# Linear attention and a squared-ReLU MLP on one core: MLP batches of 576 columns in fixed slots with attention pieces, instead of attention first and MLP in chunks of 512

## The chip, the cores and the metric

The kernel runs on one core of a Trainium2 chip. The metric is the device time of one execution in microseconds (us); the median of three runs of the kernel before is 393.43 us (390.52 to 395.26). The engines are TensorE (PE for its matmuls, PEld for its weight loads), VectorE (DVE), ScalarE (ACT), GpSimd (POOL) and SyncE (SP). SP and POOL issue the DMAs here; the data itself is moved by 16 DMA engines.

## The reference

Linear attention over 8 batches, 8 heads, 576 positions and head size 64, and then an MLP over the 4608 tokens with 512 model and 2048 inner columns:

```
theta = pi/2 * pos / S;  c, s = cos(theta), sin(theta)
phi(x) = concat(relu(x)*c, relu(x)*s)            # 64 -> 128 features
q_p, k_p = phi(q), phi(k)
kv  = einsum('bhsf,bhsd->bhfd', k_p, v)           # 128 x 64 per head
z   = sum(k_p, axis=2)
x   = (q_p @ kv) / (q_p @ z + 1e-6)               # heads side by side: 4608 x 512
out = relu(x @ w_in)**2 @ w_out                   # 512 -> 2048 -> 512
```

All inputs and the output are float32 in HBM; the kernel multiplies in bfloat16 and adds up in float32.

## The kernel before, in words

The program is written as two loops, one over the 8 batches of attention (`attention_batch`, L138) and one over 9 chunks of 512 tokens of the MLP (`mlp_chunk`, L277). Its framework orders the instructions by priority, so MLP chunks start as soon as their columns of `xT` are there, and both are mixed until the attention runs out.

A batch has 576 positions: four slices of 128 rows (position 4p+j is row p of slice j) and a tail slice of 64 rows. `attention_batch` loads K, V and Q by SP (L141 to L192), each a block of 1 MB and a tail of 128 KB. Per slice it makes the features of K, the cosine half on DVE (L167) and the sine half on ACT (L175), and casts V on ACT into `vext` (L181), which has a column of ones beside each head so that z comes out of the same matmul. For each head the five slices are then added up in PSUM by five matmuls in a row (kz, L203), and the sums are copied to `kvz` (L210). Per slice of Q it makes the features (L215, L223), transposes the 8 heads on TensorE against an identity (tps, L231), copies them out of PSUM (qpT, L235), multiplies by `kvz` (numh, L244, 65 columns per head, in two halves of 4 heads), divides (L252 adds epsilon, L259 inverts, L260 multiplies) and transposes the result in four blocks on TensorE again (L268) into `xT` (L273). `xT` holds all 4608 columns.

`mlp_chunk` computes 16 blocks of 128 inner columns (hps, L283, four matmuls of 512 columns each), applies relu on ACT (rt, L291) and squares on DVE (gT, L292). Then four output tiles of 128 tokens each take 16 matmuls of 512 columns (yps, L298), a copy on ACT (ysb, L306) and a store by SP (L313).

The weights are loaded and cast to bfloat16 by two DMAs of POOL at the very start (L104, L107). PSUM has two buffers for each of the four uses. SP issues its DMAs in order, so that a load which waits for its buffer holds up the ones behind it.

Of the kernel before, what the change touches and what calls it, by code (L numbers as in the profile page):

```python
# [9 lines left out]
ALU = mybir.AluOpType  # L11
ACTF = mybir.ActivationFunctionType
# [3 lines left out]
TOK_CHUNK = 512  # L16
EPS = 1e-06
PS_SMALL_BUFS = 2
PS_T_BUFS = 2
PS_H_BUFS = 2  # L20
PS_Y_BUFS = 2
ROWS_PER_PART = 4
# [3 lines left out]
def kernel(  # L26
# [12 lines left out]
    assert P == 128 and H * D == 512 and D == 64  # L39
    F = 2 * D  # L40
    DM, DFF = moe_w_in.shape
    T = B * S
    NB = DM // P
    KB = NB
    HB = DFF // P
    CH = max(c for c in range(P, TOK_CHUNK + 1, P) if T % c == 0)
    assert T % CH == 0 and CH % P == 0
    NCH = T // CH
    NTT = CH // P
    HH = H // 2  # L50

    J = min(ROWS_PER_PART, S // P)
    assert J >= 1
    MAIN = J * P
    TAIL = S - MAIN
    assert 0 <= TAIL < P
    NSL = J + (1 if TAIL > 0 else 0)
# [3 lines left out]
    xpool = ctx.enter_context(tc.tile_pool(name="xTp", bufs=1))  # L61
    inp = ctx.enter_context(tc.tile_pool(name="inp", bufs=2))
    kvb = ctx.enter_context(tc.tile_pool(name="kvb", bufs=2))
    qwork = ctx.enter_context(tc.tile_pool(name="qwork", bufs=2))
    small = ctx.enter_context(tc.tile_pool(name="small", bufs=2))
    mlp = ctx.enter_context(tc.tile_pool(name="mlp", bufs=2))
    ypool = ctx.enter_context(tc.tile_pool(name="ypool", bufs=2))
    ps_small = ctx.enter_context(
        tc.tile_pool(name="ps_small", bufs=PS_SMALL_BUFS, space=bass.MemoryType.PSUM)
    )  # L70
    ps_t = ctx.enter_context(tc.tile_pool(name="ps_t", bufs=PS_T_BUFS, space=bass.MemoryType.PSUM))
    ps_h = ctx.enter_context(tc.tile_pool(name="ps_h", bufs=PS_H_BUFS, space=bass.MemoryType.PSUM))
    ps_y = ctx.enter_context(tc.tile_pool(name="ps_y", bufs=PS_Y_BUFS, space=bass.MemoryType.PSUM))

    ident = const.tile([P, P], BF16, name="ident")
    make_identity(nc, ident)
    sidx = const.tile([P, J + 1], F32, name="sidx")
    nc.gpsimd.iota(
        sidx[:, 0:J],
        pattern=[[1, J]],  # L80
        base=0,
        channel_multiplier=J,
        allow_small_or_imprecise_dtypes=True,
    )
    nc.gpsimd.iota(
        sidx[:, J : J + 1],
        pattern=[[1, 1]],
        base=MAIN,
        channel_multiplier=1,
        allow_small_or_imprecise_dtypes=True,  # L90
    )
    cos_col = const.tile([P, J + 1], F32, name="cos_col")
    sin_col = const.tile([P, J + 1], F32, name="sin_col")
    bias_pi2 = const.tile([P, 1], F32, name="bias_pi2")
    nc.vector.memset(bias_pi2, math.pi / 2.0)
    theta_scale = (math.pi / 2.0) / S
    nc.scalar.activation(
        cos_col, sidx, ACTF.Sin, bias=bias_pi2[:], scale=-theta_scale
    )
    nc.scalar.activation(sin_col, sidx, ACTF.Sin, bias=0.0, scale=theta_scale)  # L100
# [3 lines left out]
    nc.gpsimd.dma_start(  # L104
        out=w1sb[:, :, :], in_=moe_w_in.rearrange("(kb p) f -> p kb f", p=P)
    )
    nc.gpsimd.dma_start(  # L107
        out=w2sb[:, :, :], in_=moe_w_out.rearrange("(hb p) f -> p hb f", p=P)
    )

    xT = xpool.tile([P, NB, T], BF16, name="xT")

    slices = [(j, P) for j in range(J)] + ([(J, TAIL)] if TAIL > 0 else [])

    def xT_dest(b, j, rows):
        c0 = b * S + (j * P if j < J else MAIN)
        return xT[:, :, c0 : c0 + rows]

    def col_to_token_pieces(c0: int, n: int):
        pieces = []  # L120
        col = c0
        end = c0 + n
        while col < end:
            b = col // S
            u = col - b * S
            if u >= MAIN:
                cnt = min(end - col, S - u)
                pieces.append((col - c0, b * S + u, 1, cnt))
                col += cnt
            else:  # L130
                j = u // P
                p0 = u % P
                cnt = min(end - col, P - p0)
                pieces.append((col - c0, b * S + J * p0 + j, J, cnt))
                col += cnt
        return pieces

    def attention_batch(b: int):  # L138
        Kb = inp.tile([P, H, J, D], F32, name="Kb", tag="Kb", bufs=2)
        Vb = inp.tile([P, H, J, D], F32, name="Vb", tag="Vb", bufs=2)  # L140
        nc.sync.dma_start(  # L141
            out=Kb[:, :, :, :],
            in_=k[b, :, 0:MAIN, :].rearrange("h (p j) d -> p h j d", j=J),
        )
        nc.sync.dma_start(
            out=Vb[:, :, :, :],
            in_=v[b, :, 0:MAIN, :].rearrange("h (p j) d -> p h j d", j=J),
        )
        if TAIL > 0:
            Kt = inp.tile([P, H, D], F32, name="Kt", tag="Kt", bufs=2)  # L150
            Vt = inp.tile([P, H, D], F32, name="Vt", tag="Vt", bufs=2)
            nc.sync.dma_start(
                out=Kt[:TAIL],
                in_=k[b, :, MAIN:S, :].rearrange("h p d -> p h d"),
            )
            nc.sync.dma_start(  # L156
                out=Vt[:TAIL],
                in_=v[b, :, MAIN:S, :].rearrange("h p d -> p h d"),
            )

        kp = kvb.tile([P, NSL, H, F], BF16, name="kp", tag="kp", bufs=2)
        vext = kvb.tile([P, NSL, H, D + 1], BF16, name="vext", tag="vext", bufs=2)
        nc.vector.memset(vext[:, :, :, D : D + 1], 1.0)
        for j, rows in slices:
            ksrc = Kb[:rows, :, j, :] if j < J else Kt[:rows, :, :]
            vsrc = Vb[:rows, :, j, :] if j < J else Vt[:rows, :, :]
            nc.vector.tensor_scalar(  # L167
                out=kp[:rows, j, :, 0:D],
                in0=ksrc,
                scalar1=0.0,  # L170
                scalar2=cos_col[:rows, j : j + 1],
                op0=ALU.max,
                op1=ALU.mult,
            )
            nc.scalar.activation(  # L175
                out=kp[:rows, j, :, D:F],
                in_=ksrc,
                func=ACTF.Relu,
                scale=sin_col[:rows, j : j + 1],
            )  # L180
            nc.scalar.copy(out=vext[:rows, j, :, 0:D], in_=vsrc)  # L181

        Qb = inp.tile([P, H, J, D], F32, name="Qb", tag="Qb", bufs=1)
        nc.sync.dma_start(
            out=Qb[:, :, :, :],
            in_=q[b, :, 0:MAIN, :].rearrange("h (p j) d -> p h j d", j=J),
        )
        if TAIL > 0:
            Qt = inp.tile([P, H, D], F32, name="Qt", tag="Qt", bufs=2)
            nc.sync.dma_start(  # L190
                out=Qt[:TAIL],
                in_=q[b, :, MAIN:S, :].rearrange("h p d -> p h d"),  # L192
            )

        kvz = kvb.tile([P, H, D + 1], BF16, name="kvz", tag="kvz", bufs=2)
        for half in range(2):
            kz = ps_small.tile(
                [P, HH, D + 1], F32, name="kz", tag="psm", bufs=PS_SMALL_BUFS
            )
            for hh in range(HH):  # L200
                h = half * HH + hh
                for ji, (j, rows) in enumerate(slices):
                    nc.tensor.matmul(  # L203
                        out=kz[:, hh, :],
                        lhsT=kp[:rows, j, h, :],
                        rhs=vext[:rows, j, h, :],
                        start=(ji == 0),
                        stop=(ji == len(slices) - 1),
                    )
            nc.scalar.copy(out=kvz[:, half * HH : half * HH + HH, :], in_=kz[:, :, :])  # L210

        for j, rows in slices:
            qsrc = Qb[:rows, :, j, :] if j < J else Qt[:rows, :, :]
            qp = qwork.tile([P, H, F], BF16, name="qp", tag="qp", bufs=2)
            nc.vector.tensor_scalar(  # L215
                out=qp[:rows, :, 0:D],
                in0=qsrc,
                scalar1=0.0,
                scalar2=cos_col[:rows, j : j + 1],
                op0=ALU.max,  # L220
                op1=ALU.mult,
            )
            nc.scalar.activation(  # L223
                out=qp[:rows, :, D:F],
                in_=qsrc,
                func=ACTF.Relu,
                scale=sin_col[:rows, j : j + 1],
            )
            tps = ps_t.tile([P, H, P], BF16, name="tps", tag="tps", bufs=PS_T_BUFS)
            for h in range(H):  # L230
                nc.tensor.transpose(  # L231
                    tps[:, h, :rows], qp[:rows, h, :], ident[:rows, :rows]
                )
# [81 lines left out]
    for b in range(B):  # L315
        attention_batch(b)
    for c in range(NCH):
        mlp_chunk(c)
# [30 lines left out]
```

## Time and profile before

| what | value |
|---|---|
| median of three runs | 393.43 us (390.52 to 395.26) |
| span of the profiled execution, first to last instruction | 388.8 us |
| granted TensorE clock, mean | 0.973 of full |
| TensorE, VectorE, ScalarE busy | 335.3, 173.0, 185.3 us |
| matmuls | 2272: 1152 of the MLP, 1120 of attention |
| DMA packets | 45755, 42.32 MB, mean 109 GB/s |

The profiled execution's own time is not listed apart from its span; the three runs lie 1.7 to 6.5 us above that span, the median 4.6. Busy time of TensorE is the union of its matmuls, of which each is recorded with its way through the array (about 0.2 us more than its step to the next one), so the step between starts is the better measure of cost. "Releaser" is what ended an engine's wait. A few per cent of the matmul records are missing.

### The profile page before, as it was taken

What the parts mean: (1) busy time and instruction counts of PE and PEld (TensorE: products, weight loads), DVE (VectorE), ACT (ScalarE), POOL (GpSimd) and SP (SyncE); (2) the same over time, 40 slices, a digit from 0 to 9 for tenths busy, and PEclk for the clock granted to TensorE, in tenths of its full rate; (3) what the DMA queues carried; (4) which work ended last, traced back from release to release, by engine and by line L of the source; (5) the groups of instructions that cost most, each with busy time, mean ns of one, the idle gap of its engine ahead of it and who ended that gap; (6) DMA issues with size and microseconds to landing.
All of it is one profiled execution on the core that took longest, in us unless ns stands there. A gap on an engine that the chain in (4) does not pass through costs nothing.

```text
span 388.8 us, 5849 instructions
## 1 busy us (share of the span) xinstructions
PE 335.3 (86%) x2272; PEld 173.0 (44%) x2272; DVE 173.0 (44%) x553; ACT 185.3 (48%) x319; POOL 2.9 (1%) x10
## 2 busy tenths in 40 slices
PE   0014586999999797999999999999999999999995
PEld 0013444565555454655544444444444444444442
DVE  1002757879687888584870150240330420420410
ACT  1063718689565758323642461551551642633621
POOL 3000000000000000000000000000000000000000
PEclk9999999899899698999999999999999999999999
DMA  8999861958859424242001101202102103002013
GB/s 218 225 214 304 258 200 25 362 198 253 248 166 306 131 78 139 65 127 66 1 2 52 57 0 54 56 0 64 46 0 83 27 6 77 28 27 79 4 27 83
DMA packets 45755, 42.32 MB, mean 109 GB/s; under 512 B 13984, under 2 KB 40608, under 8 KB 45728
## 3 DMA queue, kind: packets, MB, share of 16 engines
q1 hardware_dynamic: 43136, 37.76, 32.7%
q0 software_dynamic: 2592, 4.19, 5.8%
q8 instruction: 18, 0.29, 0.3%
q14 instruction: 9, 0.07, 0.1%
HBM read 36.70 MB, written 9.44 MB: 119 GB/s over the span
## 4 chain that ended last, share of the span: by engine, by line
PE 79%; DVE 8%; DMA 6%; SPq 2%; issue 2%; ACT 1%; ACTq 0%
PE yps L298 32%; PE hps L283 31%; DMA Qb<-in_q_dram 6%; PE tps L231 5%; PE kz L203 4%; PE tps L268 3%; PE numh L244 3%; DVE qpT L235 2%; SPq L156 2%; DVE attn L260 1%; DVE kp L167 1%; DVE qp L215 1%; DVE xT L273 1%; DVE den L252 1%; ACT vext L181 1%
## 5 line engine op out<-in xcount | busy, mean ns | idle before, releaser
L283 PE MATMUL hps<-xT,w1sb 128*128 128x512 bf16 x576 | 138.2, 389 | 0.5 <-DVE xT L273 0.5
L298 PE MATMUL yps<-w2sb,gT 128*128 128x512 bf16 x576 | 132.7, 382 | 1.6 <-DVE gT L292 0.8
L292 DVE TENSOR_TENSOR gT<-rt 128x512 bf16<-128x512 bf16 x144 | 60.4, 420 | 129.3 <-ACT rt L291 128.3
L291 ACT ACTIVATE rt<-hps 128x512 bf16<-128x512 f32 x144 | 85.3, 596 | 46.9 <-PE hps L283 45.0
L298 PEld LDWEIGHTS <-gT 128*128 128x128 bf16 x576 | 55.2, 98 | 63.8 <-issue 1.8
L283 PEld LDWEIGHTS <-w1sb 128*128 128x128 bf16 x576 | 55.3, 100 | 61.9 <-issue 4.6
L306 ACT COPY ysb<-yps 128x512 f32<-128x512 f32 x36 | 21.0, 585 | 84.0 <-PE yps L298 83.8
L203 PE MATMUL kz<-vext,kp 128*128 128x65 bf16 (+1 forms) x320 | 26.4, 204 | 27.7 <-ACT kp L175 22.5
L223 ACT ACTIVATE qp<-Qb,sin_col 128x512 bf16<-128x512 f32 x32 | 22.9, 719 | 27.8 <-PE tps L231 13.3
L203 PEld LDWEIGHTS <-kp 128*128 128x128 bf16 (+1 forms) x320 | 18.5, 100 | 34.6 <-ACT kp L175 24.6
L231 PE MATMUL tps<-ident,qp 128*128 128x128 bf16 (+1 forms) x320 | 29.3, 236 | 4.1 <-ACT qp L223 4.1
L260 DVE TENSOR_TENSOR attn<-numh,rden 128x256 bf16<-128x256 f32 (+1 forms) x80 | 32.1, 414 | 0.2
L268 PE MATMUL tps<-ident,attn 128*128 128x128 bf16 (+1 forms) x160 | 23.2, 232 | 9.6 <-DVE attn L260 9.4
L235 DVE COPY qpT<-tps 128x1024 bf16<-128x1024 bf16 (+1 forms) x40 | 25.3, 634 | 11.8 <-PE tps L231 11.3
L181 ACT CAST vext<-Vb 128x512 bf16<-128x512 f32 x32 | 18.4, 611 | 18.6 <-DMA Vb<-in_v_dram 18.6
L231 PEld LDWEIGHTS <-qp 128*128 128x128 bf16 (+1 forms) x320 | 21.9, 109 | 5.8 <-ACT qp L223 4.2
L268 PEld LDWEIGHTS <-attn 128*128 128x128 bf16 (+1 forms) x160 | 12.5, 103 | 25.8 <-DVE attn L260 17.6
L244 PE MATMUL numh<-kvz,qpT 128*128 128x65 bf16 (+1 forms) x320 | 18.7, 204 | 5.7 <-DVE qpT L235 5.7
L244 PEld LDWEIGHTS <-qpT 128*128 128x128 bf16 (+1 forms) x320 | 14.8, 107 | 19.0 <-DVE qpT L235 15.3
L175 ACT ACTIVATE kp<-Kb,sin_col 128x512 bf16<-128x512 f32 x32 | 21.7, 713 | 0.5 <-DMA Kb<-in_k_dram 0.5
L273 DVE COPY xT<-tps 128x512 bf16<-128x512 bf16 (+1 forms) x40 | 15.8, 394 | 11.5 <-PE tps L268 11.3
L215 DVE TENSOR_SCALAR qp<-Qb,cos_col 128x512 bf16<-128x512 f32 x32 | 15.1, 476 | 10.4 <-DMA Qb<-in_q_dram 10.4
(24 smaller groups left out, 74.0 us busy)
## 6 DMA issues: line engine op xcount, KB each, us to landing
Kb<-in_k_dram SPq DMA_DIRECT2D x8, 1024.0 KB, 7.8
Vb<-in_v_dram SPq DMA_DIRECT2D x8, 1024.0 KB, 10.8
Qb<-in_q_dram SPq DMA_DIRECT2D x8, 1024.0 KB, 5.5
out_dram<-ysb SPq DMA_DIRECT2D x40, 128.0 KB, 2.3
out_dram<-ysb SPq DMA_DIRECT2D x16, 256.0 KB, 2.4
w1sb<-in_moe_w_in_dram POOLq DMA_DIRECT2D x1, 2048.0 KB, 17.9
w2sb<-in_moe_w_out_dram POOLq DMA_DIRECT2D x1, 2048.0 KB, 32.2
Kt<-in_k_dram SPq DMA_DIRECT2D x8, 128.0 KB, 8.9
```

The lines of the kernel that those rows point to most:

```text
L181: nc.scalar.copy(out=vext[:rows, j, :, 0:D], in_=vsrc)
L203: nc.tensor.matmul(out=kz[:, hh, :], lhsT=kp[:rows, j, h, :], rhs=vext[:rows, j, h, :], start=(ji == 0), stop=(ji == len(slices) - 1),)
L223: nc.scalar.activation(out=qp[:rows, :, D:F], in_=qsrc, func=ACTF.Relu, scale=sin_col[:rows, j : j + 1],)
L231: nc.tensor.transpose(tps[:, h, :rows], qp[:rows, h, :], ident[:rows, :rows])
L235: nc.vector.tensor_copy(out=qpT[:, :, :rows], in_=tps[:, :, :rows])
L244: nc.tensor.matmul(out=numh[:rows, hh, :], lhsT=qpT[:, h, :rows], rhs=kvz[:, h, :], start=True, stop=True,)
L260: nc.vector.tensor_tensor(out=attn[:rows, half * HH : half * HH + HH, :], in0=numh[:rows, :, 0:D], in1=rden[:rows].unsqueeze(2).to_broadca ...
L268: nc.tensor.transpose(tps2[:, blk, :rows], attn[:rows, 2 * blk : 2 * blk + 2, :], ident[:rows, :rows],)
L283: nc.tensor.matmul(out=hps[:, :], lhsT=w1sb[:, kb, hb * P : (hb + 1) * P], rhs=xT[:, kb, t0 : t0 + CH], start=(kb == 0), stop=(kb == KB - 1),)
L291: nc.scalar.activation(out=rt[:, :], in_=hps[:, :], func=ACTF.Relu)
L292: nc.vector.tensor_tensor(out=gT[:, hb, :], in0=rt[:, :], in1=rt[:, :], op=ALU.mult)
L298: nc.tensor.matmul(out=yps[:, :], lhsT=gT[:, hb, tt * P : (tt + 1) * P], rhs=w2sb[:, hb, :], start=(hb == 0), stop=(hb == HB - 1),)
```

## The change

The whole of it is written out in one fixed order per engine (`manual_schedule`), which is the program's own.

The MLP goes by batches of 576 columns. A *slot* is a piece of MLP on TensorE. Batch b has nine slots of gemm1: four for columns 0 to 255 (four inner blocks each, matmuls of 256 columns), four for columns 256 to 511, one for the tail (16 inner blocks, matmuls of 64 columns). Each has one relu and one square over 1024 columns. Then come eight slots of gemm2 (8 matmuls of 512 columns, half an output tile each); the tails of batches 2i and 2i+1 share one output tile, in two further slots after the odd one. Batch 0 adds up four output tiles at once, so that it can use the second weight piece by piece. After each slot stand the attention pieces that a plan puts there: features of K and V casts, kz in two parts, features of Q, num with its division, all for the batch one or two ahead. For batch b from 4 on, with o and p the first slots of batches b-2 and b-1: K and V features at slots o+9 to o+11, kz at o+12 and o+13, Q features at o+13 to o+15, num and division at p+4 to p+8.

Further edits:

- kz runs slice by slice over all heads, in one PSUM buffer of two banks that num and the transposes of x share.
- num and division are done for all 8 heads at once (one of each DVE instruction instead of two).
- The transposes of Q's features and of x stay on TensorE for batches 0 and 1. For batches 2 to 7 they are DMAs issued by SP, one for a pair of slices and one for the tail: six a batch.
- V's cast moves from ACT to DVE; the copy out of the x transposes that stay on TensorE moves from DVE to ACT.
- K, V and Q of batch 0 come first, on SP. A copy of one head of V on POOL stands ahead of the weights, which come in four pieces each: the first weight, batch 1 (q, k, v), the second weight, batch 2, all on POOL. Batch 3 follows on POOL at slot 15. From batch 4 on, SP loads K and V at slot 35 or at slot 15 of batch b-3, and Q at o+9.
- Output stores go by POOL, those of the last batch by SP.
- Matmuls without a use (`warm`, `fill`) run on TensorE while it waits at the start.

The diff, cut to its core:

```diff
-    nc.gpsimd.dma_start(
-        out=w1sb[:, :, :], in_=moe_w_in.rearrange("(kb p) f -> p kb f", p=P)
-    )
...
+    def att_kv(b, part):
...
+        for j, rows in slices[:2] if part == 0 else slices[2:]:
             for hh in range(HH):
...
+                for half in range(2):
                     h = half * HH + hh
                     nc.tensor.matmul(
+                        out=kz[:, half, hh * E1 : (hh + 1) * E1],
+                        lhsT=kp[:rows, j, h, :],
+                        rhs=vx[:rows, j, h, :],
+                        start=(j == 0 and hh == 0),
+                        stop=(j == J and hh == HH - 1),
                     )
...
+    def att_qT(b, i):
...
+        nc.sync.dma_start_transpose(
+            out=t[:, :, :], in_=qps[b, i][:rows].rearrange("p r h f -> p (r h f)")
+        )
...
+    def att_num(b, j, early=False):
...
+            num = ps_a.tile([P, 2, FP], F32, name="num", tag="pa", bufs=1)
...
+    def att_x(b, i):
...
+        nc.sync.dma_start_transpose(
+            out=xT.rearrange("p k (r c) -> p (k r) c", r=n),
+            in_=xs[b, i][:rows].rearrange("p k r c -> p (k r c)"),
+        )
...
+    def gemm1(b, s):
...
+        half = s // 4
+        w, nh = (2 * P, 4) if half < 2 else (TAIL, HB)
+        h0 = s % 4 * nh
+        hps = ps_h.tile([P, nh, w], F32, name="hps", tag="hps", bufs=2)
+        xT = xT_of(b, half)
...
+        step = P if (b, s) == (0, 0) else w
+        for c in range(0, w, step):
+            for i in range(nh):
+                hb = h0 + i
+                for kb in range(KB):
+                    nc.tensor.matmul(
+                        out=hps[:, i, c : c + step],
+                        lhsT=w1sb[:, kb, hb * P : (hb + 1) * P],
+                        rhs=xT[:, kb, c : c + step],
+                        start=(kb == 0),
+                        stop=(kb == KB - 1),
+                    )
+        rt = mlp.tile([P, nh, w], BF16, name="rt", tag="rt", bufs=2)
+        nc.scalar.activation(out=rt[:, :, :], in_=hps[:, :, :], func=ACTF.Relu)
...
+    def gemm2(b, s):
...
+        tt, part = divmod(s, 2)
+        if part == 0:
+            yps = ps_y.tile([P, DM], F32, name="yps", tag="yps", bufs=2)
+            ypss[b] = yps[:, :]
+        for hb in range(part * HB // 2, (part + 1) * HB // 2):
+            gemm2_mm(b, tt, hb, ypss[b])
+        if part == 1:
+            store(b, tt, ypss[b])
...
+    at(15, load_batch, 3, nc.gpsimd, "qkv")
+    plan(
+        2,
+        k=(26, 26, 27, 27, 28),
+        f=(18, 20, 22, 26, 26),
+        kv=(29, 29),
+        d=(30, 31, 32, 33, 34),
+    )
...
+    for b in range(4, B):
+        o, p = first[b - 2], first[b - 1]
+        at(35 if b == 4 else first[b - 3] + 15, load_batch, b, nc.sync, "kv")
+        at(o + 9, load_batch, b, nc.sync, "q")
+        plan(
+            b,
+            k=(o + 9, o + 9, o + 10, o + 10, o + 11),
+            f=(o + 13, o + 13, o + 14, o + 14, o + 15),
+            kv=(o + 12, o + 13),
+            d=[p + 4 + j for j in range(NS)],
+        )
+
+    def run(s):
+        fn, b, i = slots[s]
+        rest = fn(b, i)
+        for fn2, args in after.get(s, []):
+            fn2(*args)
+        if rest:
+            rest()
...
+    with tc.manual_schedule():
+        load_batch(0, nc.sync, "kvq")
+        constants()
...
+        att_v(0, J - 1, nc.gpsimd, H - 1, H)
...
+        for i in range(4):
+            load_w1(i, 4)
+        load_batch(1, nc.gpsimd, "qkv")
+        for i in range(4):
+            load_w2(i, 4)
+        load_batch(2, nc.gpsimd, "qkv")
+        att_kv(0, 0)
+        att_kv(0, 1)
...
+        for s in range(len(slots)):
+            run(s)
```

`run` issues a slot's matmuls and relu, then its attention pieces, then its square.

More of the change, by code (lines that the diff above doesn't have):

```diff
@@ L6 @@
 import concourse.tile as tile
-from concourse import bass_utils, mybir
+from concourse import mybir
 from concourse._compat import with_exitstack
@@ L138, in attention_batch @@
[L138 to L143, printed above, removed]
-        )
-        nc.sync.dma_start(
-            out=Vb[:, :, :, :],
-            in_=v[b, :, 0:MAIN, :].rearrange("h (p j) d -> p h j d", j=J),
-        )
[L149 to L154, printed above, removed]
-            )
-            nc.sync.dma_start(
-                out=Vt[:TAIL],
-                in_=v[b, :, MAIN:S, :].rearrange("h p d -> p h d"),
-            )
[L161 to L199, printed above, removed]
-            for hh in range(HH):
[L201 to L233, printed above, removed]
-            qpT = qwork.tile([P, H, P], BF16, name="qpT", tag="qpT", bufs=2)
-            nc.vector.tensor_copy(out=qpT[:, :, :rows], in_=tps[:, :, :rows])
-            attn = qwork.tile([P, H, D], BF16, name="attn", tag="attn", bufs=2)
-            for half in range(2):
-                numh = ps_small.tile(
-                    [P, HH, D + 1], F32, name="numh", tag="psm", bufs=PS_SMALL_BUFS
-                )
-                for hh in range(HH):
@@ new lines, in att_qT_pe @@
+    def att_qT_pe(b, j, apart=False):
+        rows = slices[j][1]
+        tq = ps_y.tile([P, H, P], BF16, name="tq", tag="yps", bufs=2)
+        if apart:
+            hi = ps_h.tile([P, HH, P], BF16, name="tqh", tag="hps", bufs=2)
+        else:
+            hi = tq[:, HH:H, :]
+        tqs[b, j] = [tq[:, 0:HH, :], hi]
+        for h in range(H):
+            nc.tensor.transpose(
+                tqs[b, j][h // HH][:, h % HH, :rows], qp_of(b, j)[:rows, h, :], ident[:rows, :rows]
+            )
@@ new lines, in att_qT_copy @@
+    def att_qT_copy(b, j, both=False):
+        rows = slices[j][1]
+        qpTs[b, j] = [
+            att.tile([P, HH, P], BF16, name=f"qpTp{i}", tag=f"qpTp{i}", bufs=5) for i in range(2)
+        ]
+        for i, t in enumerate(qpTs[b, j]):
+            copy = nc.scalar.copy if both and i else nc.vector.tensor_copy
+            copy(out=t[:, :, :rows], in_=tqs[b, j][i][:, :, :rows])
+    def att_num(b, j, early=False):
+        rows = slices[j][1]
+        qpT, kvz = qpTs[b, j], kvzs[b]
+        if early:
+            num = ps_h.tile([P, 2, FP], F32, name="num", tag="hps", bufs=2)
+        else:
+            num = ps_a.tile([P, 2, FP], F32, name="num", tag="pa", bufs=1)
+        for h in range(H):
+            e0 = (h % HH) * E1
+            nc.tensor.matmul(
+                out=num[:rows, h // HH, e0 : e0 + E1],
+                lhsT=qpT[h // HH][:, h % HH, :rows],
+                rhs=kvz[:, h, :],
+                start=True,
+                stop=True,
+            )
+        nums[b, j] = num
@@ new lines, in store @@
+    def store(b, tt, acc):
+        ysb = mlp.tile([P, DM], F32, name="ysb", tag="ysb", bufs=4)
+        nc.scalar.copy(out=ysb[:, :], in_=acc)
+        eng = nc.sync if b == B - 1 else nc.gpsimd
+        if tt < J:
+            rows = [(0, P, b * S + tt, J)]
+        else:
+            rows = [(k * TAIL, TAIL, (b - 1 + k) * S + MAIN, 1) for k in range(2)]
+        for p0, n, row0, step in rows:
+            dst = bass.AP(tensor=out.tensor, offset=row0 * DM, ap=[[step * DM, n], [1, DM]])
+            eng.dma_start(out=dst, in_=ysb[p0 : p0 + n, :])
@@ new lines, with at, att_d, att_t @@
+    NS = J + 1
+    slots, first = [], {}
+    for b in range(B):
+        first[b] = len(slots)
+        slots += [(gemm1, b, i) for i in range(9)]
+        slots += [(gemm2, b, i) for i in range(2 * J + (2 if b % 2 else 0))]
+    after = {}
+    def at(s, fn, *args):
+        after.setdefault(s, []).append((fn, args))
+    def att_d(b, j):
+        att_num(b, j)
+        att_div(b, j)
+    def att_t(b, j):
+        att_qT_pe(b, j)
+        att_qT_copy(b, j)
+    def att_v_dve(b, j):
+        att_v(b, j, nc.vector)
```

423 lines of the change are left out of this document (279 added, 144 removed).

## Prediction

> **What bounds the kernel now.** I read the page first, then busy time by stretches, the waits of TensorE, the chain of waits, and last a few places of the timeline for the price of each kind of matmul.
>
> ```profile
> span 388.8 us, 5849 instructions
> PE 335.3 (86%) x2272; PEld 173.0 (44%) x2272; DVE 173.0 (44%) x553; ACT 185.3 (48%) x319; POOL 2.9 (1%) x10
> ```
>
> ```profile
> 0.00:22.54 22.54, 0.00 (x1) 0.01 (x1) 1.92 (x7) 2.98 (x6) 2.95 (x10) 1.00 0.97 219
> 22.54:52.40 29.86, 13.52 (x128) 9.95 (x129) 13.86 (x46) 15.80 (x27) 0.00 (x0) 1.00 1.04 280
> 52.40:162.00 109.60, 99.41 (x927) 57.93 (x926) 86.07 (x300) 74.44 (x132) 0.00 (x0) 0.92 0.58 177
> 162.00:204.80 42.80, 42.74 (x388) 23.87 (x388) 29.69 (x104) 17.77 (x30) 0.00 (x0) 0.96 0.18 51
> 204.80:384.40 179.60, 179.58 (x833) 81.22 (x830) 41.45 (x98) 73.75 (x124) 0.00 (x0) 1.00 0.15 40
> ```
>
> Columns of the second fence: stretch and its length, then busy time of PE, PEld, DVE, ACT and POOL, granted TensorE clock, DMA share, GB/s. Four stages are to be seen: 22.5 us in which TensorE has nothing, 30 us in which it is busy for less than half, 152 us in which attention and MLP are mixed, and 180 us of pure MLP without a gap at clock 1.00.
>
> A busy TensorE isn't one at its peak, so I price each kind of matmul by the step from one start to the next. A group of n that lasts L, with about 0.2 us for one of it, has the step (L - 0.2)/(n - 1).
>
> ```profile
> 204.81 13.81 PE yps L298 x64
> 370.57 13.83 PE yps L298 x64
> ...
> 162.28 0.27 PE L203 MATMUL kz<-vext,kp 128*128 128x65 bf16 x3
> ...
> 162.28 2.56 PE L203 MATMUL kz<-vext,kp 128*128 128x65 bf16 x34
> 164.78 0.62 PE L231 MATMUL tps<-ident,qp 128*128 128x128 bf16 x8
> 169.20 0.43 PE L244 MATMUL numh<-kvz,qpT 128*128 128x65 bf16 x8
> 178.47 0.44 PE L244 MATMUL numh<-kvz,qpT 128*64 128x65 bf16 x8
> ```
>
> - 512 columns: 13.81/64 = 0.2158 us, for both matrix products of the MLP.
> - 128 columns (transposes): (0.62 - 0.22)/7 = 0.057 us. A line through these two gives 0.110 for 256 columns.
> - 65 columns: kz 0.035, numh 0.033 us (with 64 columns of weights 0.034), though each loads weights of its own. kz adds into the same place up to five times in a row, and that costs nothing.
> - But 34 kz in a row take (2.56 - 0.2)/33 = 0.072 us each, not 0.035. Every fifth has 64 rows instead of 128, so one head takes 5 x 0.072 = 0.36 us instead of 0.175: going to the short tile and back costs about 0.1 us each time.
>
> By these steps the whole kernel needs 1152 x 0.2158 + 64 x 0.36 + 320 x 0.036 + 480 x 0.055 = 248.6 + 23.0 + 11.5 + 26 = 309 us on TensorE. The span holds 22.5 us ahead of the first matmul, 4.4 behind the last, and so 53 us of waits and slow clock, nearly all before 162 us. The longest of them:
>
> ```profile
> PE kz L203 <- ACT kp L175: 22.5, 1, 22.5
> PE tps L268 <- DVE attn L260: 9.4, 10, 1.1
> PE numh L244 <- DVE qpT L235: 5.7, 9, 1.1
> ```
>
> **The change, part by part.** The profiled execution stands at 388.8 us of span against a median of 393.4, so I work in span and add 4.6 us.
>
> *Start.* K, V and Q of batch 0 now go first on SP, and the weights wait on POOL behind a copy that reads V.
>
> ```profile
> 6.96 1.67 DVE L167 TENSOR_SCALAR kp<-Kb,cos_col 128x512 bf16<-128x512 f32 x4 [5.70 <-DMA Kb<-in_k_dram]
> 21.24 0.62 ACT L181 CAST vext<-Vb 128x512 bf16<-128x512 f32 x1 [18.59 <-DMA Vb<-in_v_dram]
> 35.31 0.88 DVE L215 TENSOR_SCALAR qp<-Qb,cos_col 128x512 bf16<-128x512 f32 x2 [10.20 <-DMA Qb<-in_q_dram]
> ...
> 2.00:6.00 4.00, 0.00 (x0) 0.00 (x0) 0.00 (x0) 0.63 (x3) 1.57 (x2) 1.00 0.91 279
> 36.00:40.00 4.00, 2.33 (x23) 1.92 (x24) 2.95 (x11) 2.62 (x6) 0.00 (x0) 1.00 1.09 385
> 40.00:42.00 2.00, 1.20 (x16) 0.94 (x13) 1.42 (x3) 1.13 (x2) 0.00 (x0) 1.00 0.68 165
> ```
>
> Before, K was there at 7 us, V only at 21 and Q at 35, since both shared the queues' turns with the weights. K, V and Q of a batch are 3 x 1.18 MB; at 279 to 385 GB/s from 2 us on, V lands at 8 to 10 us and Q at 11 to 15, or near 20 if the weights take turns with it again. kz then runs at 12 to 15 us. Behind Q come features, transposes, copies, num, division, x transposes and copy for two slices, 5 to 6 us by the durations below and the cold steps. The first MLP slot starts at 19 to 26 us; I take 21.
>
> *TensorE's work.* gemm1 on 256 columns: 1024 x 0.110 = 112.6. Its tails, 512 matmuls of 64 columns: nearest is the 65-column step, 0.030 to 0.036, so 15 to 18; I take 16.4 (before, these columns cost 13.8). gemm2: 576 x 0.2158 = 124.3. kz now goes slice by slice over all heads, so the short tile is met once a batch and not once a head: 40 x 0.035 + 0.2 = 1.6, times 8 = 12.8, a gain of 10. num 11.5. Transposes on TensorE are left for batches 0 and 1 alone: 120 x 0.056 = 6.7, a gain of 20. Sum 284.3, of which 3.8 lie ahead of the first slot: 280.5.
>
> *What goes beside it.* Between two slots stand attention pieces, each with a change of tile and a semaphore. Bounds: nothing, and 0.25 us for each of ten pieces a batch, 20 us; the mixed stretch at 162 to 204.8 shows PE busy throughout, so I take 6. ACT and DVE must keep up:
>
> ```profile
> L291 ACT ACTIVATE rt<-hps 128x512 bf16<-128x512 f32 x144 | 85.3, 596 | 46.9 <-PE hps L283 45.0 <-DVE gT L292 0.7 <-DVE rden L259 0.5
> L292 DVE TENSOR_TENSOR gT<-rt 128x512 bf16<-128x512 bf16 x144 | 60.4, 420 | 129.3 <-ACT rt L291 128.3 <-ACT vext L181 0.8
> L260 DVE TENSOR_TENSOR attn<-numh,rden 128x256 bf16<-128x256 f32 x64 | 25.8, 415 | 0.2
> L223 ACT ACTIVATE qp<-Qb,sin_col 128x512 bf16<-128x512 f32 x32 | 22.9, 719 | 27.8 <-PE tps L231 13.3 <-DMA Qb<-in_q_dram 11.0 <-DVE xT L273 2.3
> L259 DVE RECIPROCAL rden<-den 128x4 f32<-128x4 f32 x64 | 10.2, 169 | 0.0
> L252 DVE TENSOR_SCALAR den<-numh 128x4 f32<-128x4 f32 x64 | 9.1, 159 | 4.9 <-PE numh L244 3.9
> ```
>
> A batch takes TensorE 280.5/8 = 35 us. ACT has 9 relus of 1024 (at most 2 x 0.596), ten features of 0.72, five output copies and one of kvz: 22 us. DVE has 9 squares (0.84), ten features, five V copies and five divisions: about 21. Both fit. The tight place is the five gemm1 slots that carry a division: DVE 0.16 + 0.17 + 2 x 0.415 + 0.84 = 2.0 us against 16 x 0.110 + 8 x 0.033 = 2.02 on TensorE.
>
> *Transposes by DMA.* From batch 2 on a batch sends 1.77 MB of qp and x through SP in six DMAs, in order with its loads. The trace holds no transposing DMA. As large pieces at 385 GB/s they would take 4.6 us a batch, as small pieces at 165 GB/s (40 to 42 us, where the 128 KB tails go in rows of 256 B) 10.7; with 3.5 MB of loads (9 us) and 1.2 MB of stores (3 us) that is 17 to 23 us of the DMA engines in 35. Latency: x of a pair leaves five slots (9 us) ahead of its use in batch 2 and twelve later. So I price them at nothing; the cover is these slots, and gone it costs what the rival below says.
>
> *Weights.* First 2 MB, then batch 1, then the second 2 MB, on POOL.
>
> ```profile
> w1sb<-in_moe_w_in_dram POOLq DMA_DIRECT2D x1, 2048.0 KB, 17.9
> w2sb<-in_moe_w_out_dram POOLq DMA_DIRECT2D x1, 2048.0 KB, 32.2
> ```
>
> Both together took 32 us beside other loads, so about 13 each alone. From 11 us: w1 until 24 to 29, batch 1 until 33 to 44, w2 until 46 to 58. TensorE asks for the first piece of w2 near 43 us and for the last near 53. Late by 0 to 15 us; I take 4.
>
> *End.*
>
> ```profile
> 384.46 0.59 ACT L306 COPY ysb<-yps 128x512 f32<-128x512 f32 x1 [2.87 <-PE yps L298]
> ```
>
> The same copy and store stand last: 4.4 us. **Sum:** 21 + 280.5 + 6 + 4 + 4.4 = 316 us of span, 320 with 4.6 around it.
>
> **The rivals.**
>
> *DVE paces the division slots.* num has a single PSUM buffer, so slot s+1 can't write num before the division of s is through, and that division stands behind a square. If a slot loses 0.5 us, 5 x 8 x 0.5 = 20 us: 340. For it: 2.0 against 2.02. Against it: 30 of 35 us where DVE is slack.
>
> *Loads arrive late at the start.* w2 and batch 2 come 15 us late instead of 4, the start at 26 instead of 21: 336. For it: a DMA share near 1 up to 52 us. Against it: the order asks for less at a time.
>
> *The clock.* If unbroken work brings the 0.92 of 52 to 162 us, 280.5/0.92 adds 24: 344. Against it: 1.00 through 180 us of unbroken matmuls.
>
> *Transposing DMAs are slow; the other side.* Neighbouring elements of a row go to different partitions. If that splits the writes, the DMA engines bound six batches. Pieces of 64 B that each take as long as one of 256 B would move 165/4 = 41 GB/s: 43 us a batch, 55 with loads and stores, and 50 us ahead of them, six batches and a last MLP of 35 give 50 + 6 x 55 + 35 = 415, 420 with 4.6: slower. It decides from 39 us a batch (50 + 6 x 51 + 35 = 391) on; half as bad, 30 us, gives 50 + 6 x 42 + 35 = 337, 342 in all. For it: no row prices such a write. Against it: up to 23 us a batch it is hidden altogether, a margin of two over the row for small pieces.
>
> The Trainium skill differs from itself on this. Its page "VectorE: DVE Perf Modes", section "The three transpose paths", gives 1309 ns for a 128x128 block by DMA against 390 by TensorE; a batch's 51 blocks one behind the other would be 67 us, an estimate, and the sum 50 + 6 x 79 + 35 = 559, deep in the slower case. Its page "DMA: Bandwidth & Descriptors", section "Latency and other measured facts", gives 261 GB/s for a transposing DMA, 6.8 us a batch, an estimate, which would be hidden and leave the sum as it is. The trace shows neither; it shows TensorE's transposes at a step of 57 ns.
>
> *The change does less than it says:* TensorE is spared 25 us of work (309 to 284) and waits as long as before: 393 - 25 = 368. For it: fixed slots are still a chain of waits. Against it: the waits quoted above are on features and division of the same slice, and the slots put a whole slot of MLP between such steps.
>
> **How the numbers follow.** The forecast 0.68; DVE 0.10; loads 0.08; clock 0.03; slow transposes 0.08, of which 0.05 slower than before; less than it says 0.03. The forecast's own ends: with kz and tails at 0.030, 19 + 276 + 0 + 0 + 4.4 + 4.6 = 304, and 26 + 282 + 14 + 8 + 4.4 + 4.6 = 339. The range 304 to 346 takes in the first, the loads, the clock and most of DVE. A measurement here tells about 1% from no change; faster by that 0.93, within it 0.02, slower 0.05.
>
> **What would show it.** Right: first MLP matmul near 21 us; TensorE without gaps over 0.3 us from 60 us on; groups of 64-column matmuls at 0.03 us; kz at 1.6 us a batch; no wait of TensorE on a DMA behind 60 us. Wrong: TensorE waiting for qpT or xT from a DMA in batches 2 to 7; num waiting for the division; granted clock under 0.97 behind 60 us; gemm1 steps over 0.115.

## The result, and the profile after

The changed kernel takes 303.95 us (median of 4 runs, 303.73 to 304.23) against 391.98 us before: ratio 0.7755, interval 0.7712 to 0.7797. The forecast was 320 with a range of 304 to 346, so the direction and most of the size were right and the time lies 0.05 us under the lower end. The profiled execution took 304.11 us, with a span of 302.3.

The head of the page of the changed kernel:

```profile
span 302.3 us, 6836 instructions
PE 289.0 (96%) x2911; PEld 201.7 (67%) x2911; DVE 140.3 (46%) x330; ACT 157.8 (52%) x214; POOL 42.5 (14%) x69
PE   0899999999999999999999999999999999999993
PEclk9999999999999999999999999999999999999998
```

TensorE is busy in every slice from the second to the last but one, at a granted clock of 0.9 or more. The stretches, with the columns as in the prediction, cut at the first MLP slot, at 60 us and at the tail slots of batches 2 and 4 (two stretches between them look the same and are left out):

```profile
0.00:19.86 19.86, 11.07 (x111) 6.27 (x112) 8.69 (x24) 10.79 (x18) 8.72 (x18) 1.00 0.97 240
19.86:60.00 40.14, 40.14 (x464) 30.16 (x462) 22.79 (x56) 23.54 (x35) 14.81 (x20) 1.00 1.09 303
60.00:111.23 51.23, 51.23 (x563) 38.19 (x562) 32.23 (x78) 32.43 (x45) 3.93 (x8) 1.00 0.74 181
...
179.87:297.80 117.93, 117.90 (x1096) 78.81 (x1092) 43.06 (x95) 53.02 (x68) 8.64 (x14) 1.00 0.43 112
```

Behind 19.86 us there is no stretch in which TensorE is idle. All its waits on other engines, over the whole execution:

```profile
PE wm L185 <- ACT kp L163: 7.2, 1, 7.2
PE kz L214 <- DVE vext L177: 1.0, 1, 1.0
PE num L277 <- ACT qpTp L266: 0.2, 1, 0.2
```

All three lie ahead of the first slot. Of the 86.5 us of span that are gone (388.8 - 302.3), 53 are the waits and the slow clock of the old mixed stage, 6 the start (22.5 us; now 19.9, in which 3.8 us of work are done) and 27 work that TensorE no longer has (309 us; now 277.9 behind the start and those 3.8). How the 53 us divide among the edits is not shown: no kernel here leaves the fixed order out. The steps of its matmuls, from the chain of waits (MLP) and from the timeline (attention):

```profile
280.51 17.28 PE yps L384 x80
128.82 8.73 PE hps L351 x80
143.82 1.87 PE hps L351 x64
```

```profile
120.32 0.65 PE L214 MATMUL kz<-vext,kp 128*128 128x65 bf16 x16
120.81 1.89 PE L384 MATMUL yps<-w2sb,gT 128*128 128x512 bf16 x8
122.54 1.00 PE L214 MATMUL kz<-vext,kp 128*128 128x65 bf16 x24
123.47 0.82 PE L384 MATMUL yps<-w2sb,gT 128*128 128x512 bf16 x3
```

17.28/80 = 0.216 us for 512 columns, 8.73/80 = 0.109 for 256, 1.87/64 = 0.029 for 64. kz takes 0.49 and 0.93 us to the start of the next group, 1.42 a batch. num takes 0.26 us a slice and 0.38 for the tail. Counted out behind the first slot, 1008 matmuls of 256 columns (110.0 us), 32 of 128 (1.8), 512 of 64 (15.0), 576 of 512 (124.4), kz of seven batches (9.9), 38 num (10.8) and the 88 transposes that are left (4.6, an estimate from 0.056 for a full one) make 276.5 of the 277.9 us.

The transposing DMAs, and a stretch in which only one of them, for an x pair, moved data (last columns: DMA share, GB/s):

```profile
qpT<-qp SPq DMA_TRANSPOSE x12, 3.9
xT<-x SPq DMA_TRANSPOSE x12, 3.4
qpT<-qpt SPq DMA_TRANSPOSE x6, 3.5
xTt<-xt SPq DMA_TRANSPOSE x6, 2.3
```

```profile
246.00:249.00 3.00, 3.00 (x58) 2.81 (x56) 2.31 (x8) 1.74 (x2) 0.00 (x0) 1.00 0.48 92
```

A pair of slices lands 3.4 to 3.9 us behind its issue. 92 GB/s at a share of 0.48 is 192 GB/s of a full share: by this, an estimate, 1.77 MB would hold the DMA engines for 9.2 us a batch, between the 4.6 and 10.7 of the prediction, and with loads and stores for some 21 of 35.

### The profile page after: what moved, and what is told of

Same layout as the page of the kernel before. It is cut to its first block, busy times and chain, and to the rows that moved or that the text cites. A ratio compares the mean times of both kernels' runs of the same rounds, so it can differ in the third digit from the quotient of the medians.

```text
span 302.3 us, 6836 instructions
## 1 busy us (share of the span) xinstructions
PE 289.0 (96%) x2911; PEld 201.7 (67%) x2911; DVE 140.3 (46%) x330; ACT 157.8 (52%) x214; POOL 42.5 (14%) x69
## 4 chain that ended last, share of the span: by engine, by line
PE 93%; DMA 3%; SPq 1%; ACT 1%; DVE 0%; issue 0%; ACTq 0%
PE hps L351 42%; PE yps L384 39%; PE num L277 4%; PE kz L214 3%; DMA q<-in_q_dram 3%; PE yh L384 2%; PE tq L255 1%; SPq L69 1%; PE tx L323 1%; PE wm L197 0%; ACT qpTp L266 0%; SPq L65 0%; DVE qp L153 0%; ACT ysb L372 0%; PE tqh L255 0%
## 5 line engine op out<-in xcount | busy, mean ns | idle before, releaser
L351 PEld LDWEIGHTS <-w1sb 128*128 128x128 bf16 x1552 | 114.2, 98 | 12.4
L351 PE MATMUL hps<-xT,w1sb 128*128 128x256 bf16 (+1 forms) x1040 | 117.7, 271 | 0.0
L384 PE MATMUL yps<-w2sb,gT 128*128 128x512 bf16 x480 | 109.4, 379 | 0.0
L359 ACT ACTIVATE rt<-hps 128x1024 bf16<-128x1024 f32 x72 | 73.7, 1024 | 59.4 <-DVE gT L366 32.8
L366 DVE TENSOR_TENSOR gT<-rt 128x1024 bf16<-128x1024 bf16 x64 | 44.0, 687 | 83.8 <-ACT rt L359 83.8
L372 ACT COPY ysb<-yps 128x512 f32<-128x512 f32 x34 | 19.9, 589 | 57.2 <-PE yps L384 57.2
L380 POOL DMA_DIRECT2D out_dram<-ysb x34 | 20.6, 609 | 187.1 <-ACT ysb L372 187.1
L163 ACT ACTIVATE qp<-q,sin_col 128x512 bf16<-128x512 f32 x32 | 21.9, 717 | 4.1 <-DMA q<-in_q_dram 4.1
L163 ACT ACTIVATE kp<-k,sin_col 128x512 bf16<-128x512 f32 x32 | 21.2, 715 | 3.5 <-DMA k<-in_k_dram 3.5
L295 DVE TENSOR_TENSOR x<-num,rden 128x512 bf16<-128x512 f32 x32 | 22.1, 692 | 1.1
L351 PE MATMUL hps<-xTt,w1sb 128*128 128x64 bf16 x512 | 16.2, 193 | 0.0
```

Source lines behind the costliest of these rows:

```text
L163: nc.scalar.activation(out=dst[:rows, :, D:F], in_=src, func=ACTF.Relu, scale=sin_col[:rows, j : j + 1])
L295: nc.vector.tensor_tensor(out=x_of(b, j)[:rows].rearrange("p (b k) (l d) -> p b k l d", b=2, l=2), in0=n4[:, :, :, 0:D].rearrange("p b (k ...
L351: nc.tensor.matmul(out=hps[:, i, c : c + step], lhsT=w1sb[:, kb, hb * P : (hb + 1) * P], rhs=xT[:, kb, c : c + step], start=(kb == 0), sto ...
L359: nc.scalar.activation(out=rt[:, :, :], in_=hps[:, :, :], func=ACTF.Relu)
L366: nc.vector.tensor_tensor(out=dst, in0=rt[:, :, :], in1=rt[:, :, :], op=ALU.mult)
L372: nc.scalar.copy(out=ysb[:, :], in_=acc)
```

## The experiments

Theory: behind the start, the time is the sum of TensorE's steps, changes of tile included, and everything else is hidden. Each rival says that something else holds it up, or that some of TensorE's work is hidden. The kernels ran in three groups, each on one chip; the last group had the changed kernel with it. Times are set against 303.95 us, in the last group against 303.84.

**Transposes of batches 4 to 7 back on TensorE.**

```diff
-            d=[p + 4 + j for j in range(NS)],
+            d=(p + 2, p + 4, p + 6, p + 8, p + 10),
+            t=(p, p + 1, p + 2, p + 3, p + 5),
+            x=(p + 3, p + 5, p + 7, p + 9, p + 11),
```

> The changed kernel with the transposes of qp and x of batches 4 to 7 on TensorE again, as it does them for batch 1, in place of 24 transposing DMAs. Theory (TensorE's steps alone make the time behind 20 us): each batch gets 40 transposes of qp and 20 of x back, 32 x 0.056 + 8 x 0.042 + 16 x 0.056 + 4 x 0.055 = 3.2 us, four batches 13 us, so 317 against 303.95. Rival (transposing DMAs hold up something themselves, so that leaving them out gives time back): under 312. Rival (the copies out of PSUM load DVE and ACT so far that they pace): over 321.

317.63 us, 13.7 more; the theory said 13. (num and division also move, to every second slot.) So the DMAs take this work off TensorE at no price of their own, and the extra copies out of PSUM are hidden.

**kz head by head in its second part.**

```diff
-        for j, rows in slices[:2] if part == 0 else slices[2:]:
-            for hh in range(HH):
-                for half in range(2):
+        for hh in range(HH):
+            for half in range(2):
+                for j, rows in part_slices:
```

> The changed kernel, but in the second part of kz each head adds up its three slices before the next head begins, so that the 64-row tile is met 8 times a batch and not once. Same 320 matmuls, same sums. Theory (every TensorE step is on the path, and a change between 128 and 64 rows costs 0.095 to 0.1 us): 7 more pairs of changes a batch, 7 x 2 x 0.097 = 1.36 us, for seven batches 9.5 and up to 1.4 more at the start: 314. Rival (the slots have room beside TensorE's work, kz is hidden): 304.

317.18 us (315.64 to 318.53), 13.2 more where 10 were expected. The timeline of one batch:

```profile
126.00 0.65 PE L215 MATMUL kz<-vext,kp 128*128 128x65 bf16 x16
...
128.22 2.46 PE L215 MATMUL kz<-vext,kp 128*128 128x65 bf16 x24
130.61 4.49 PE L385 MATMUL yps<-w2sb,gT 128*128 128x512 bf16 x20
```

The 24 matmuls of the second part take 2.39 us to the start of the next group, where they took 0.93: 1.46 more. The profiled execution (315.64) is 11.5 longer, of which 1.2 is the later start (first slot at 21.03 us) and 10.3 the seven other batches, 1.47 each. So a change of tile costs 0.105 us and counts in full. Why the other three executions are up to 3 us longer than the profiled one isn't settled.

**Attention of batches 4 to 7 left out.**

```diff
-    for b in range(4, B):
+    for b in ():
...
     def xT_of(b, i):
+        b = min(b, 3)
```

> Leaves out the loads and the attention of batches 4 to 7; their MLP reads batch 3's x. Theory (a piece between two slots costs its matmuls' steps, changes of tile included, and nothing else): kz 1.41 and num 1.36 us a batch, four batches 11.1, so 293. Rival (each piece costs up to 0.1 us more for its semaphores, as the prediction allowed: 6 us over eight batches): 290. Rival (loads, transposing DMAs or DVE hold TensorE up in the steady part): under 289.

291.94 us, 12.0 less; of the 12.4 us by which the profiled span is shorter, 0.7 lie ahead of the first slot (19.18 us against 19.86). Behind it 11.7 us. A batch's pieces, by the timeline from their start to that of the next group, are kz 1.42 and num 4 x 0.26 + 0.38 = 1.42, four batches 11.4. So 28 pieces cost 0.3 us beyond their steps: 0.01 each, not the 0.075 that the prediction's 6 us came to.

**The division's multiply twice.**

```diff
+        for _ in range(2 if b >= 4 else 1):
             nc.vector.tensor_tensor(
                 out=x_of(b, j)[:rows].rearrange("p (b k) (l d) -> p b k l d", b=2, l=2),
```

> In batches 4 to 7 the division's multiply (0.69 us on DVE) is done twice, with the same result. DVE then has 0.17 + 0.20 + 2 x 0.69 + 0.69 = 2.44 us and gaps in each of the five slots with a division, TensorE 2.0. Theory (TensorE alone makes the time, and slack elsewhere takes up what DVE lacks): 304 to 305. Rival (division slots are at DVE's edge, so num waits for the division): 4 batches x 4 to 5 slots x 0.5 us, so 312 to 314.

309.60 us, 5.65 more: between the two. In the timeline num now follows at a step of 2.4 us, which is DVE's sum of 2.44, and it waits for DVE:

```profile
139.24 0.43 PE L277 MATMUL num<-kvz,qpT 128*128 128x65 bf16 x8 [0.20 <-DVE x L296]
141.71 0.42 PE L277 MATMUL num<-kvz,qpT 128*128 128x65 bf16 x8 [0.29 <-DVE x L296]
144.07 0.43 PE L277 MATMUL num<-kvz,qpT 128*128 128x65 bf16 x8 [0.20 <-DVE x L296]
```

In the changed kernel the same step is 2.0 us, with no wait:

```profile
139.39 0.42 PE L277 MATMUL num<-kvz,qpT 128*128 128x65 bf16 x8
...
141.40 0.42 PE L277 MATMUL num<-kvz,qpT 128*128 128x65 bf16 x8
```

DVE needs 0.17 + 0.20 + 0.69 + 0.69 = 1.75 there, so the slots had 0.25 us to spare, where the prediction had 0.02. Square and multiply of twice the size cost 0.69 and not twice 0.42:

```profile
L366 DVE TENSOR_TENSOR gT<-rt 128x1024 bf16<-128x1024 bf16 x64 | 44.0, 687 | 83.8 <-ACT rt L359 83.8
L295 DVE TENSOR_TENSOR x<-num,rden 128x512 bf16<-128x512 f32 x32 | 22.1, 692 | 1.1
```

**The first weight ahead of everything on POOL.**

```diff
         constants()
+        for i in range(4):
+            load_w1(i, 4)
...
-        att_v(0, J - 1, nc.gpsimd, H - 1, H)
```

> The changed kernel with the first weight's four DMAs at the head of POOL's queue and without the copy of V on POOL that holds them back; all later loads follow at once. Theory (the start is set by Q of batch 0, and Q lands late when its packets take turns with the weights'): in the kernel before, Q landed at 35 us; here about 30, so the first MLP slot stands at 30 to 36 us in place of 19.9, and the time is 314 to 320. Rival (the same bytes have to come anyway, and what comes earlier of the weights and of batch 1 is won back): 304 to 308.

323.70 us, 19.75 more. The first slot starts at 39.54 us instead of 19.86, 19.7 later, and the rest takes as long as before: from there to the start of the last matmul 277.5 us in both. TensorE waits for V and Q:

```profile
PE tq L255 <- ACT qp L163: 8.5, 1, 8.5
PE wm L185 <- DVE kp L153: 7.6, 1, 7.6
PE kz L214 <- DVE vext L177: 6.8, 2, 5.3
```

ACT gets Q at 31.7 us there, at 14.0 in the changed kernel, and SP issues it at 5 us in both. So the order of the loads at the start (the first weight and batch 1 held back until V is there) is worth 20 us, more than a fifth of the whole gain, and nothing of what comes earlier is won back.

**Without the matmuls that have no use.**

```diff
-            if j < J:
-                warm(0, j)
...
-        for j in range(J):
-            warm(0, j)
...
-            fill(4 - j)
```

> The changed kernel without the matmuls that have no use (16 at kz, 7 at the x transposes of batch 0). Theory (they keep the clock up, and without them the first 3 to 4 us of matmuls run at about half speed, as at 26 to 60 us of the kernel before, where transposes stepped by 107 ns): about 0.9 us for transposes and num and 1.8 in the first MLP slots, 306 to 307. Rival (they are only filling): 304.

305.77 us, 1.8 more, a little less than the theory's 306 to 307. The first slot starts at 20.88, 1.0 later, where 0.9 was expected; but its 32 matmuls take 2.59 us and not 1.95, 0.6 more, where 1.8 was expected of the first slots:

```profile
20.07 1.01 PE L255 MATMUL tq<-ident,qp 128*128 128x128 bf16 x8
20.88 2.59 PE L351 MATMUL hps<-xT,w1sb 128*128 128x128 bf16 x32
```

The clock column doesn't show this: it says 1.00 from 10 to 24 us of this kernel, though four transposes take 0.43 us from 15.40 on, 0.107 each instead of 0.056. Here the slow rate is read from the steps alone.

**The tail slice at full size.** kz, num and the transposes of qp use 128 rows of the tail, of which 64 are zeros that are set once.

```diff
-        for j, rows in slices[:2] if part == 0 else slices[2:]:
+        for j, rows in [(j, P) for j, _ in (slices[:2] if part == 0 else slices[2:])]:
...
+        nc.gpsimd.memset(kp0[TAIL:P, J, :, :], 0.0)
```

> The changed kernel with the tail slice at full size for kz, num and the transposes of qp: its upper 64 rows are zeros that are set once, so that these matmuls keep 128 rows and 128 columns of weights. Theory (TensorE's steps make the time, and going to a smaller tile and back costs 0.19 us): two such changes fewer a batch, 8 x 2 x 0.19 = 3.0, so 301. Rival (a change of tile is hidden between slots): 304. Rival (the transposing DMA of the tail, twice as large, is late): over 304.

300.52 us (ratio to before 0.7640, 0.7597 to 0.7683), 3.4 less than the changed kernel; the theory said 3.0. Its four runs (299.84 to 301.92) lie below all eight of the changed kernel (302.86 to 304.23). More work by columns, less time.

```profile
120.97 0.89 PE L226 MATMUL kz<-vext,kp 128*128 128x65 bf16 x24
121.70 4.48 PE L396 MATMUL yps<-w2sb,gT 128*128 128x512 bf16 x20
```

The second part of kz takes 0.73 us instead of 0.93.

**And both ends shortened.** Q of batch 0 in two halves, the last tile alone and copied by two engines.

```diff
+        for j in (0, 2):
+            nc.sync.dma_start(out=main[:, :, j : j + 2, :], in_=rows[:, :, j : j + 2, :])
...
+            tt = (0, 1, 2, J, J - 1)[tt]
...
+            for c, copy, eng in [(0, nc.vector.tensor_copy, nc.sync), (hw, nc.scalar.copy, nc.scalar)]:
+                copy(out=ysb[:, c : c + hw], in_=acc[:, c : c + hw])
```

> As with full-height tails, and also: Q of batch 0 in two DMAs, so that its first two slices come earlier, with their first features ahead of the copy of kvz; the last batch's shared tail tile ahead of its fourth output tile; the last tile copied half on DVE and half on ACT, each half with a DMA of its own from SP and ACT. Theory (the chain at both ends counts in full): 0.5 us at the start, 0.8 at the end (one store less in the row, half a copy), so 299.8. Rival (the start hangs on kvz and the end on the store's landing alone): within 0.3 us of the full-height tails alone.

300.09 us (299.78 to 300.43), ratio 0.7625 (0.7580 to 0.7670): the fastest here of the kernels that do all the work, but only 0.4 us ahead of the tails alone, whose runs (299.84 to 301.92) overlap with it. The first slot starts 0.28 us earlier (19.42 against 19.70), the end comes 0.3 sooner behind the last matmul: together 0.6 of the 1.3 us that were expected. The two half copies don't run side by side:

```profile
294.17 0.42 DVE L396 COPY ysb<-yps 128x256 f32<-128x256 f32 x1 [15.58 <-PE yps L414]
294.62 0.34 SPq L400 DMA_DIRECT2D out_dram<-ysb  x1
294.62 0.37 ACT L396 COPY ysb<-yps 128x256 f32<-128x256 f32 x1 [3.38 <-DVE ysb L396]
```

**The second weight behind batch 2**, in one group with the two that follow and with the changed kernel again.

> The changed kernel once more, on the chip of the three beside it: 303.7 to 304.3.

303.84 us (302.86 to 304.12).

```diff
-        for i in range(4):
-            load_w2(i, 4)
-        load_batch(2, nc.gpsimd, "qkv")
...
+            if s == 3:
+                load_batch(2, nc.gpsimd, "qkv")
+                for i in range(4):
+                    load_w2(i, 4)
```

> The changed kernel with the second weight behind batch 2's loads on POOL and not ahead of them: it comes by about 9 us later. In the changed kernel gemm2 starts at 39.7 us without a wait. Theory (the second weight came only a few us ahead of its use, and a wait for it counts in full): its first piece lands near 46 us, so 6 us are lost and 310 is measured. Rival (it came 9 us or more ahead): 304.

316.09 us, 12.25 more. TensorE waits 8.8 us for the first piece, and the clock falls in this gap:

```profile
48.97 1.03 PE L384 MATMUL yh<-w2sb,gT 128*128 128x512 bf16 x2 [8.78 <-DMA w2sb<-in_moe_w_out_dram]
...
48.90:54.00 5.10, 5.03 (x12) 1.79 (x13) 0.00 (x0) 0.00 (x0) 0.00 (x0) 0.50 1.24 206
```

With the two behind this stretch, fourteen matmuls take 5.93 us (48.97 to 54.90), 0.424 each instead of 0.216: 2.9 us. 9.2 us of later start (48.97 against 39.74, with 0.2 from a later first slot) and 2.9 of slow clock make 12.1 of the 12.2 us by which the profiled span is longer. The Trainium skill says in "TensorE: Matmul & The Clock Gate", Part 1, that an idle window of about 3.4 us brings the array back to half rate; this trace agrees, with 8.8 us of waiting and 0.50 behind it. The theory's 6 us were too few, because the weight had come hardly ahead of its use. In the changed kernel a wait of POOL ends when the first piece lands:

```profile
38.55 0.89 POOL L65 DMA_DIRECT2D v<-in_v_dram  x1 [1.59 <-DMA w2sb<-in_moe_w_out_dram]
39.74 0.60 PE L384 MATMUL yh<-w2sb,gT 128*128 128x512 bf16 x2
```

That is 1.2 us ahead of the matmul that needs it. With the loads moved, the piece lands about 10.4 us later, and 9.2 of them are lost.

**x just in time, and too late.** num and division of batches 4 to 7 eight slots later, and ten (`p + 14 + j`); both parts of kz in one slot.

```diff
-            kv=(o + 12, o + 13),
-            d=[p + 4 + j for j in range(NS)],
+            kv=(o + 12, o + 12),
+            d=[p + 12 + j for j in range(NS)],
```

> For batches 4 to 7 num and division stand eight slots later (p+12 to p+16, with both parts of kz in one slot), so that the first x pair's transposing DMA is issued 4 or 6 slots (8 to 12 us) ahead of its use and not 12 or 14. Theory (the DMA needs 3.4 us and the division 1.2, which 8 us still hide): 304. Rival (transposing DMAs are late in the queue of SP behind loads): over 306.

> The same two slots later still (p+14 on), so that for batches 5 and 7 the first x pair is divided two slots ahead of its use. Theory (division 1.2 and transposing DMA 3.4 us against one slot of 2.0 us in between, and TensorE waits for the rest): 2.6 to 3 us each for two batches, so 309 to 310. Rival (transposing DMAs finish much sooner than their issue-to-landing time says): 304 to 305.

314.23 and 323.29 us, 10.4 and 19.45 more. The first of these expectations failed. TensorE's waits in it:

```profile
PE kz L214 <- DVE x L295: 3.9, 3, 1.3
PE hps L351 <- DMA xTt<-xt: 3.3, 2, 3.0
PE hps L351 <- DMA xT<-x: 0.3, 1, 0.3
```

It wasn't the first pair that came late, which the 8 us did hide (the 0.3 us are for a second pair), but the tail of batch 5, nine slots ahead of its use: SP issued it behind another batch's K and V.

```profile
206.90 0.58 SPq L65 DMA_DIRECT2D k<-in_k_dram  x1
207.53 0.65 SPq L69 DMA_DIRECT2D kt<-in_k_dram  x1
208.22 0.72 SPq L65 DMA_DIRECT2D v<-in_v_dram  x1
208.99 2.75 SPq L69 DMA_DIRECT2D vt<-in_v_dram  x1
211.83 2.90 SPq L310 DMA_TRANSPOSE xTt<-xt  x1
```

A further 3.9 us are the edit's own: num now shares its PSUM buffer with a kz that stands in the same slots. These 7.5 us are the waits as listed. From step to step each of the six takes 0.17 to 0.18 us more, 1.0 in all, and behind the wait of 3.0 us the clock was low:

```profile
218.30:220.70 2.40, 2.33 (x64) 2.34 (x64) 0.00 (x0) 0.00 (x0) 0.00 (x0) 0.78 1.09 369
220.70:228.70 8.00, 8.00 (x37) 3.49 (x35) 4.35 (x11) 4.67 (x7) 0.54 (x1) 0.85 0.14 44
```

The 64 matmuls of 64 columns and 32 of 512 that start there take 10.4 us instead of 8.8, 1.6 more. Together that is 10.1 of the 10.2 us by which the span is longer.

Two slots later, TensorE waits six times for x pairs, 13.9 us in all and up to 4.2 at once, in batches 4 and 6 too, where only 5 and 7 were expected to. So the transposes are hidden in the changed kernel by their place in SP's queue as much as by the slots that lie in between.

## Why the prediction was right, and where it was wrong

The mechanism was right: from the first slot on, the time is TensorE's steps. The step for 256 columns, which it had no row for, held (0.109 for 0.110); 64 columns (0.029 for 0.030 to 0.036) and kz (1.42 us for 1.6) came out smaller. But the forecast was 16 us too long. Three terms of its sum were too large: the 4.6 us around the span (measured 1.8), which also set the range too high, the 6 us for what goes beside TensorE's work (0.01 us a piece) and the 4 us for a late second weight (no wait). 21 + 280.5 + 6 + 4 + 4.4 + 4.6 = 320 became, in the profiled execution, 19.9 + 277.9 + 0 + 0 + 4.5 + 1.8 = 304.1. By its own steps:

- *"I work in span and add 4.6 us."* This failed, and it alone put the lower end of the range too high. Each execution of either kernel lies 1.7 to 1.9 us above its own span: of the kernel before, 390.37 us with 388.6, 395.73 with 393.9. The other 2.8 us were the scatter of the kernel before, from 389 to 396 us, whose profiled execution was one of the short ones. The changed kernel doesn't scatter so: 302.86 to 304.23 in eight runs. With 1.8 the forecast's own lower end would have been 301. That this end still came within 0.05 us of the measured time is luck: its start of 19 and its work of 276 us were 2.8 us too short together, as much as the 4.6 was too long. Why the kernel before scatters isn't settled.
- *"Bounds: nothing, and 0.25 us for each of ten pieces a batch ... I take 6."* It was the lower bound: 0.01 us a piece, by the kernel without the attention of four batches.
- *"Late by 0 to 15 us; I take 4."* The lower bound again, but only by luck: by POOL's wait the first piece landed 1.2 us ahead of its use, and in the kernel where it came 10.4 us later, 9.2 us were lost.
- TensorE's work 277.9 and not 280.5: tails 8 x 1.87 = 15.0 for 16.4, kz 7 x 1.42 = 9.9 for 11.2 behind the start.
- *"I take 21"*: 19.9. V was there at 10.9 us, a little behind the 8 to 10, and Q at 14.0, inside 11 to 15.
- *DVE paces the division slots*: no, with 0.25 us to spare a slot. DVE's work was taken too high by doubling rows of half the size (0.83 and 0.84 for 0.69 each).
- *Transposing DMAs priced at nothing*: right, and 13.7 us is what four batches of them are worth. Its bound of 10.7 us a batch was misread: 165 GB/s at a share of 0.68 is 243 of a full share, or 7.3 us, so the 9.2 us lie above what its rows for plain pieces bound. A batch also has 54 blocks of 32 KB, not 51. As to the two figures of the Trainium skill: 16 blocks of 128x128 landed 3.9 us behind their issue, 0.24 us a block, so the 1309 ns of "VectorE: DVE Perf Modes" isn't a price for blocks in a row; the 192 GB/s here is about a quarter under the 261 GB/s of "DMA: Bandwidth & Descriptors".
- *The clock*: 1.00 in every stretch shown above, 0.996 in the mean.

Two allowances, 6 and 4 us, each taken between a bound of nothing and a large one, were both nothing. Against the first stood a row of the prediction itself: in the mixed stretch from 162 to 204.8 us TensorE was busy for 42.74 of 42.80 us, with attention pieces between the MLP's matmuls.

## What to carry to other kernels

Where an engine is to be kept full, price its work by the steps from start to start of dense stretches, and then look for what can leave a gap: the order of the first loads (20 us here), a weight moved behind another load (12 us, a quarter of it by the clock), a DMA behind others in its queue. Tile shape has a price of its own: going from 128 to 64 rows and back costs as much as seven small matmuls, so that padding with zeros was faster than the smaller tile. Before adding what lies around the span, compare execution with its own span, not with a median.

## What was not expected of the hardware

A transposing DMA moves 192 GB/s of a full DMA share, little more than half of the 353 of plain loads in the kernel before (385 GB/s at a share of 1.09). A matmul of 64 columns with its own weights steps by 29 ns, while a change between 128 and 64 rows costs 105 ns. One gap of 9 us cost 2.9 us more in clock, and one of 3.0 us still cost 1.6. And with the first weight and batch 1's loads let in at once, Q of 1.18 MB, issued at 5 us in both kernels, came 17.7 us later; the DMA share was 1.05 to 1.18 from 6 to 32 us, so Q shared full DMA engines with those loads. The clock column said 1.00 at the start of a kernel even where the steps were twice as long (0.107 us for 128 columns without the useless matmuls).
